# One multiply of the polynomial exponential of chunk 53 is issued behind the pair's normalisation on VectorE

## The chip, the cores and the metric

The kernel runs on one core of a Trainium2 chip. The metric is the device time of one execution in microseconds (us). A core has a matrix engine (PE in the profile), a vector engine (DVE), a scalar engine (ACT), GpSimd (POOL) and a queue engine that issues transfers (SP). Each engine runs its own instructions in the order in which they were issued, and semaphores order them between engines.

## What is computed

Attention with a soft cap on the scores, over 8 batches and 12 heads of 448 tokens with 64 dimensions, followed by a soft mixture of experts over the 3584 tokens with 768 dimensions: 32 slots, 8 experts with a hidden layer of 1024.

```python
scores = scale * np.matmul(q, k.transpose(0, 1, 3, 2))
scores = cap * np.tanh(scores / cap)
attn = np.exp(scores - max)
attn = attn / (np.sum(attn, axis=-1, keepdims=True) + 1e-09)
attn_out = np.matmul(attn, v)
...
logits = x @ phi
d = softmax(logits, over tokens); slot_input = d.T @ x
h = np.maximum(slot_input[e] @ w1[e], 0.0); slot_out[e] = h @ w2[e]
out = softmax(logits, over slots) @ slot_out
```

## The kernel before

Heads are taken in pairs, 48 in all, and four heads (two pairs) share one load of q, k and v. The scores of a pair are 7 tiles; the 336 tiles of all pairs are put into one sequence in which neighbouring pairs interleave, and the sequence is cut into 56 chunks of 6 tiles. A chunk has two halves of three tiles. For each half PE computes scores into one of two score buffers (L349), and ACT takes the tanh of them into the chunk's tile `ex` (L366, or L362 for both halves at once). Then ACT takes the exponential in place (L374), but not of all tiles: in the chunks listed in `SHARED` the first one to three tiles are left to DVE, which works out the exponential with a polynomial in seven operations.

These seven are the steps 0 to 6 of `poly_exp`: scale to a fixed-point exponent (L601), take its fraction (L603), square it (L604), scale and add (L605), multiply by the fraction (L606), add to the exponent (L607), scale to the bits of a bf16 number (L608). The steps of one chunk use a scratch tile `xf` (written by L603) and a scratch tile `xp` (written by L604 to L606). There is one of each, so chunks that are in work at the same time take turns. Chunk 52 has one such tile (448 elements), chunk 53 has three (1344), chunk 54 has one.

The place of each step on DVE is written out by hand in `POLY`: a key (j, slot) names the turn j of the main loop over chunks and a slot in it, and the value lists (chunk, step). `run(j, slot)` issues what a slot holds, first its part marked `<`, then the plain part (other work that was planned there), then the part marked `>`. One turn j of the main loop issues, in this order: slot 0, the tanh of the first half, slot m, the tanh of the second half, slot e, the exponential of chunk j - 1, then, where a pair has its last tile in chunk j - 2, the first matmuls of the probabilities with the values for that pair (`pv_first`, four of its seven tiles), slot a, the score matmuls of the next first half, slot b, the remaining matmuls and the normalisation (`pv_rest`, which calls `norm`), the cast of later values (`vcast_after`), slot c, the score matmuls of the next second half, slot d.

`norm` is a reciprocal of the row sums (L633, into `rec`) and a multiply (L636, into `xq`), both on DVE. They read the PSUM bank `pv`, of which there is one: the next pair's `pv_first` writes the same bank and waits until L636 has read it. The bank also takes filler matmuls (`spare`, `fill`) between pairs.

`vcast_after` is on GpSimd: a cast of loaded values to bf16 (L289, into `vbd`), after every other pair with a small memset (L297) ahead of it. It writes a tile that the pair's matmuls have read, so the last of these releases it, as it releases `norm`.

In turn 53 the slot '>a' holds step 5 of chunk 52 and step 2 of chunk 53 (L604), slot c holds `slot_sums` (whose DVE part is L777, into `slacc`), slot '>c' step 6 of chunk 52 and step 3 of chunk 53. Turn 54 goes on with the steps 4 and 5 of chunk 53 and the first steps of chunk 54 and closes the next pair. Turn 55 is the last; behind it a written-out sequence (`TAILSEQ`) ends the attention of the last two pairs (`pvm`, `pvl`), then come the slot sums, the two expert layers (L1071, L1099) and the output stage (L1139 to L1193), whose rows are stored by transfers that SP issues (L1127).

## Time and profile before

| | us |
|---|---|
| median of 3 runs | 283.83 |
| lowest and highest of them | 283.61, 285.08 |
| profiled execution | 282.72 |
| its span | 280.7 |

The profile shows one execution. Its span reaches from the first to the last instruction recorded; the execution's own time is 2.0 us longer. The mean granted clock of PE is 0.988 of full speed. Rows of the order of time give start, duration, engine, line, operation, output <- inputs and, in brackets, the idle time of the engine before it with what ended it. "xN" merges N instructions that follow each other. On DVE a row's duration reaches about 0.08 us into the next row. The chain of waits follows the work that ended last back to what released it.

### The profile page before, as it was taken

Reading aid. Unit: us, or ns where it says so; the run is one execution under the profiler, and the core shown is the slowest. Engines: PE = TensorE matmul, PEld = TensorE weight load, DVE = VectorE, ACT = ScalarE, POOL = GpSimd, SP = SyncE. Lnnn points to the kernel's source line nnn. Section 1 sums busy time; section 2 is a strip of 40 time slices with the busy share of each in tenths; the row PEclk is TensorE's granted clock in tenths of the full one; section 3 lists DMA queues with packets and bytes.
Section 4 is the critical chain, followed back from the end, with each engine's and each line's share of the span. In section 5 each row is a group of like instructions: output and inputs, shape, how many; then the busy total and the mean of one; then the engine's idle time right before and its main releaser. Section 6 shows DMA issues by size and latency. Waiting matters only on the chain.

```text
span 280.7 us, 10442 instructions
## 1 busy us (share of the span) xinstructions
PE 247.1 (88%) x4561; PEld 166.3 (59%) x4561; DVE 239.8 (85%) x474; ACT 248.8 (89%) x196; POOL 142.0 (51%) x198
## 2 busy tenths in 40 slices
PE   8898989998999999989999999899998989997720
PEld 6555556756675667566657675667565758652410
DVE  3479999999999999999999999999999996457840
ACT  4999999999999999999999999999999997236730
POOL 7976548663956296628663858295734120200000
PEclk9999999999999999999999999999999999999995
DMA  7999999999999999999999999999999468969997
GB/s 230 270 190 204 220 218 226 233 219 216 213 226 220 219 226 230 219 217 230 231 217 209 224 224 224 215 209 216 228 216 217 135 231 279 409 271 381 413 421 308
DMA packets 58332, 68.08 MB, mean 243 GB/s; under 512 B 4144, under 2 KB 54448, under 8 KB 58288
## 3 DMA queue, kind: packets, MB, share of 16 engines
q0 software_dynamic: 42448, 35.31, 79.7%
q1 hardware_dynamic: 15552, 31.89, 32.2%
q8 instruction: 35, 0.57, 0.7%
q10 hardware_dynamic: 288, 0.23, 0.3%
q14 instruction: 9, 0.07, 0.1%
HBM read 91.72 MB, written 19.27 MB: 395 GB/s over the span
## 4 chain that ended last, share of the span: by engine, by line
ACT 38%; DVE 31%; PE 23%; issue 4%; POOL 0%; DVEq 0%; ACTq 0%
ACT ex L366 15%; ACT ex L374 15%; PE pv L626 6%; ACT ex L362 6%; DVE xq L636 5%; DVE xp L604 4%; DVE xp L606 3%; DVE ex L607 3%; PE sc L349 2%; DVE ex L601 2%; DVE xf L603 2%; DVE ex L608 2%; DVE xp L605 2%; PE so_ps L1099 2%; DVE qT L281 2%
## 5 line engine op out<-in xcount | busy, mean ns | idle before, releaser
L366 ACT ACTIVATE ex<-sc 128x1344 f16<-128x1344 f32 (+1 forms) x87 | 112.7, 1399 | 1.4 <-PE sc L349 1.4
L374 ACT ACTIVATE ex<-ex 128x1344 bf16<-128x1344 f16 (+5 forms) x58 | 110.5, 1908 | 0.1
L626 PE MATMUL pv<-vbd,ex 128*128 128x130 bf16 (+1 forms) x1610 | 93.9, 212 | 8.7 <-DVE xq L636 4.2
L626 PEld LDWEIGHTS <-ex 128*128 128x128 bf16 (+1 forms) x1680 | 75.6, 101 | 35.8 <-issue 6.2
L289 POOL CAST vbd<-vraw 64x896 bf16<-64x896 f32 x46 | 47.6, 1034 | 56.7 <-PE pv L626 44.5
L349 PE MATMUL sc<-qT,kT 64*64 64x448 bf16 x672 | 66.1, 359 | 6.5 <-ACT ex L366 4.7
L362 ACT ACTIVATE ex<-sc 128x2688 f16<-128x2688 f32 x13 | 33.6, 2586 | 0.0
L349 PEld LDWEIGHTS <-kT 64*64 64x64 bf16 x672 | 22.0, 105 | 16.3 <-ACT ex L366 6.8
L636 DVE TENSOR_TENSOR xq<-pv,rec 128x448 bf16<-128x448 f32 x46 | 28.7, 625 | 1.6
L604 DVE TENSOR_TENSOR xp<-xf 128x1344 f16<-128x1344 uint16 (+2 forms) x34 | 27.5, 810 | 0.2
L606 DVE TENSOR_TENSOR xp<-xp,xf 128x1344 f16<-128x1344 f16 (+2 forms) x34 | 27.1, 798 | 0.6
L607 DVE TENSOR_TENSOR ex<-ex,xp 128x1344 uint16<-128x1344 uint16 (+2 forms) x34 | 26.9, 791 | 0.2
L116 POOL DMA_DIRECT2D w1b<-in_moe_w_dram x32 | 26.2, 822 | 0.0
L601 DVE TENSOR_SCALAR ex<-ex 128x1344 uint16<-128x1344 f16 (+2 forms) x34 | 16.8, 495 | 1.3 <-ACT ex L366 0.7
L297 POOL MEMSET vbd<- 64x1 bf16 x22 | 2.9, 131 | 29.7 <-PE pv L626 29.4
L281 DVE COPY kT<-kps 128x896 bf16<-128x896 bf16 x23 | 14.2, 618 | 4.2 <-PE kps L276 2.8
L605 DVE TENSOR_SCALAR xp<-xp 128x1344 f16<-128x1344 f16 (+2 forms) x34 | 17.1, 501 | 0.6
L185 POOL DMA_DIRECT2D qb<-in_q_dram x22 | 16.3, 739 | 2.5 <-PE qps L279 1.8
L603 DVE TENSOR_SCALAR xf<-ex 128x1344 uint16<-128x1344 uint16 (+2 forms) x34 | 16.7, 491 | 0.4
L608 DVE TENSOR_SCALAR ex<-ex 128x1344 uint16<-128x1344 uint16 (+2 forms) x34 | 16.4, 483 | 0.4
L120 POOL DMA_DIRECT2D w2d<-in_moe_w_dram x21 | 16.4, 817 | 0.0
L185 POOL DMA_DIRECT2D kb<-in_k_dram x22 | 16.3, 742 | 0.0
(124 smaller groups left out, 320.1 us busy)
## 6 DMA issues: line engine op xcount, KB each, us to landing
w1b<-in_moe_w_dram POOLq DMA_DIRECT2D x32, 384.0 KB, 9.6
vraw<-in_v_dram SPq DMA_DIRECT2D x44, 224.0 KB, 6.2
w2d<-in_moe_w_dram POOLq DMA_DIRECT2D x21, 384.0 KB, 9.5
w2t<-w2d SPq DMA_DIRECT2D x21, 384.0 KB, 6.7
out_dram<-ob SPq DMA_DIRECT2D x7, 768.0 KB, 6.6
qb<-in_q_dram POOLq DMA_DIRECT2D x22, 224.0 KB, 7.3
kb<-in_k_dram POOLq DMA_DIRECT2D x22, 224.0 KB, 7.7
w2b<-in_moe_w_dram POOLq DMA_DIRECT2D x11, 384.0 KB, 9.1
```

Of the source, the lines that this page charges most:

```text
L116: pool.dma_start(out=w1b[e][:, js, fs], in_=w1r[:, e, js, fs])
L185: pool.dma_start(out=t, in_=quad_ap(nm, Q))
L289: pool.tensor_copy(vbds[Q % 2][r, :, :, c0:c0 + DH], raw[r])
L349: ins = pe.matmul(sc[cs, u, 0:S], qkT["k", Q][r, c, cs], qkT["q", Q][r, :, cs], start=True, stop=True).ins
L362: apart["t", i - 1] = apart["t", i] = act.activation(exs[j].bitcast(F16), own["board"][:, :, 0:S], ACT.Tanh, scale=qk_scale / cap).ins
L366: ins = act.activation(exs[j][:, half * CS + u0:half * CS + u1, :].bitcast(F16), (own[0] if i == u0 == 0 else sc)[:, u0:u1, 0:S], ACT.Tanh ...
L374: act.activation(exs[j][:, u0:u1, :], exs[j][:, u0:u1, :].bitcast(F16), ACT.Exp, scale=cap)
L604: lambda: dve.tensor_tensor(p, s, s.bitcast(F16), op=ALU.mult),
L606: lambda: dve.tensor_tensor(p, p, s, op=ALU.mult),
L607: lambda: dve.tensor_tensor(y, y, p, op=ALU.add),
L626: pe.matmul(out_, exs[j][r, u, q0:q0 + (HP if tail else P)], v_, start=(c == 0 and g == gs[0] < NF), stop=(c == NT - 1), skip_group_check= ...
L636: dve.tensor_tensor(xq[Q][:, h, s0:s1, :], pv[:, 0:s1 - s0, 0:DH], rec.to_broadcast([P, s1 - s0, DH]), op=ALU.mult)
```

## The change

Step 2 of chunk 53 (the square, L604, on 128 partitions by 1344 elements) moves from slot '>a' to slot '<c' of turn 53, that is from ahead of `pv_rest` to behind it. The other entries stay.

```diff
             (53, 'm'): ((53, 0),),
             (53, 'e'): ((52, 3), (51, 6)),
             (53, '<a'): ((52, 4), (53, 1)),
-            (53, '>a'): ((52, 5), (53, 2)),
+            (53, '>a'): ((52, 5),),
+            (53, '<c'): ((53, 2),),
             (53, '>c'): ((52, 6), (53, 3)),
             (54, '<a'): ((53, 4),),
```

On DVE the order around it becomes:

```
before: L603 (53), L607 (52), L604 (53), L633, L636, L777, L608 (52), L605 (53), L606 (53)
after:  L603 (53), L607 (52), L633, L636, L604 (53), L777, L608 (52), L605 (53), L606 (53)
```

The numbers in brackets are chunks. The other engines and the transfer queues keep their order, and no wait between engines changes.

## The prediction

> **What bounds the kernel now.** I read first the busy rows of the page and the stretches of the end, then the chain of waits, then the time order of each engine around the edited place.

> ```profile
> span 280.7 us, 10442 instructions
> ...
> PE 247.1 (88%) x4561; PEld 166.3 (59%) x4561; DVE 239.8 (85%) x474; ACT 248.8 (89%) x196; POOL 142.0 (51%) x198
> ```

> ```profile
> 220.00:224.00 4.00, 3.94 (x83) 2.82 (x84) 3.90 (x12) 4.00 (x5) 1.05 (x2) 1.00 0.33 98
> 224.00:228.00 4.00, 2.95 (x73) 2.34 (x73) 3.90 (x9) 4.00 (x4) 0.93 (x1) 1.00 0.73 241
> 228.00:232.00 4.00, 3.94 (x62) 2.72 (x61) 3.92 (x10) 3.70 (x3) 1.11 (x2) 1.00 0.68 226
> 232.00:236.00 4.00, 4.00 (x92) 3.52 (x89) 3.03 (x10) 3.81 (x5) 0.00 (x0) 1.00 0.90 304
> ```

> Columns: stretch, length, busy time of PE, its weight loads, DVE, ACT and POOL, granted clock, DMA share, GB/s. Over the whole span three engines are nearly level, so the shares decide nothing. The edited operation runs in the second stretch, where PE does 2.95 us of work in 4 and DVE and ACT are full; before and after it PE is full. The granted clock is 1.00 throughout, so no clock term enters the sum. The chain of waits says what costs PE that time:

> ```profile
> 224.05 0.31 DVE ex L607
> ...
> 224.38 1.60 DVE xp L604
> 225.98 0.13 DVE rec L633
> ...
> 226.13 0.63 DVE xq L636
> 226.77 0.14 issue
> 226.91 0.84 PE pv L626 x12
> ```

> ```profile
> 223.33 0.90 PE L626 MATMUL pv<-vbd,ex 128*128 128x130 bf16 x15
> ...
> 225.29 0.57 PE L349 MATMUL sc<-qT,kT 64*64 64x448 bf16 x6
> 226.91 0.84 PE L626 MATMUL pv<-vbd,ex 128*128 128x130 bf16 x12 [1.05 <-DVE xq L636]
> ```

> The chain runs on DVE up to 226.77 and on PE from then on. At the crossing PE has finished its score matmuls (225.29 + 0.57 = 225.86) and stands still for 1.05 us: the next pair's matmuls need the bank pv, which the normalisation (rec, then xq) must have read. The bank was complete at 223.33 + 0.90 = 224.23, but rec came only at 225.9, because the edited operation, the multiply L604 of chunk 53, stood before it for 1.60 us. That duration is odd:

> ```profile
> L604 DVE TENSOR_TENSOR xp<-xf x34: 386/847/1599, 14.2 to 231.4; 128x1344 f16<-128x1344 uint16 x27, 128x896 f16<-128x896 uint16 x5, 128x448 f16<-128x448 uint16 x2
> ```

> ```profile
> 224.35 0.93 POOL L289 CAST vbd<-vraw 64x896 bf16<-64x896 f32 x1 [3.13 <-PE pv L626]
> ```

> The median of L604 is 0.85 us and this is the slowest of 34. GpSimd's cast of the values began at 224.35, 0.03 us ahead of it, and ended at 225.28; L604 ended 0.70 us behind that, about as if it had begun when the cast ended. Other meetings of the two kinds:

> ```profile
> 138.31 0.85 DVE L604 TENSOR_TENSOR xp<-xf 128x1344 f16<-128x1344 uint16 x1
> ...
> 212.50 1.07 DVE L606 TENSOR_TENSOR xp<-xp,xf 128x1344 f16<-128x1344 f16 x1
> ```

> ```profile
> 138.67 1.27 POOL L289 CAST vbd<-vraw 64x896 bf16<-64x896 f32 x1 [2.17 <-PE pv L626]
> ...
> 211.90 0.95 POOL L289 CAST vbd<-vraw 64x896 bf16<-64x896 f32 x1
> ```

> Where the multiply is already running (138.31), it keeps its 0.85 us and the cast takes 1.27; where the cast runs first (211.90 to 212.85), the multiply's end slips to 0.72 us behind the cast's end. So whichever starts first makes the other wait. The normalisation is not held by a cast: the last matmul of a pair releases both, so they meet again and again, as at 229.94 and 229.79 in rows further down, and yet the page's group of L636 has the mean 625 ns over 46.

> ```profile
> L636 DVE TENSOR_TENSOR xq<-pv,rec 128x448 bf16<-128x448 f32 x46 | 28.7, 625 | 1.6
> ```

> [...]

> **The change, part by part.** Nothing is added or removed: L604 of chunk 53 moves on DVE past rec (L633) and xq (L636) and comes ahead of slacc (L777). PE, ACT, GpSimd and the DMA queues keep their order; no DMA is moved or passed.

> ```profile
> 225.91 0.19 DVE L633 RECIPROCAL rec<-pv 128x7 f32<-128x7 f32 x1
> 226.13 0.62 DVE L636 TENSOR_TENSOR xq<-pv,rec 128x448 bf16<-128x448 f32 x1
> 226.68 0.38 DVE L777 TENSOR_TENSOR slacc<-slps,slacc 128x224 f32<-128x224 f32 x1
> ```

> (1) The normalisation. Its wait for PE was over at 224.23 and DVE is free at 224.36, so rec starts at 224.38 instead of 225.91: 1.53 us earlier. xq ends at 226.75 - 1.53 = 225.22. With the 0.14 to 0.16 us from xq's end to the first matmul, the bank is free for PE at about 225.38, before PE is done with its scores at 225.86. PE's 1.05 us go down to the 0.05 or so between two of its groups: pv starts near 225.9, 1.0 us earlier.

> (2) The multiply. Behind xq it starts near 225.14, while the cast runs until 225.28; 0.70 us behind that is 225.98, or 0.85 us by itself is 225.99. So slacc, which followed the normalisation at 226.68, now follows L604 at about 225.91, and all later work on DVE has 0.77 us in hand. Bounds of this term: 0 if L604 were held for 1.60 us again, 0.77 if not. I take 0.77, since only 0.14 us of the cast are left.

> (3) What comes back. DVE gains 0.77, PE 1.0. They meet first at the next normalisation, behind which the filler matmul and the last pairs write the same bank:

> ```profile
> 228.66 0.85 DVE L607 TENSOR_TENSOR ex<-ex,xp 128x1344 uint16<-128x1344 uint16 x1
> 229.42 0.27 DVE L603 TENSOR_SCALAR xf<-ex 128x448 uint16<-128x448 uint16 x1
> 229.70 0.21 DVE L633 RECIPROCAL rec<-pv 128x7 f32<-128x7 f32 x1
> 229.94 0.62 DVE L636 TENSOR_TENSOR xq<-pv,rec 128x448 bf16<-128x448 f32 x1
> ```

> ```profile
> 230.85 0.28 PE junk L875
> ...
> 231.18 0.84 PE pv L626 x12
> ```

> xq ends at 230.56 and frees the bank for 230.70; the chain has the filler at 230.85, so the slack is 0.15. With PE 1.0 and DVE 0.77 earlier, PE waits 1.0 - 0.77 - 0.15 = 0.08 us. PE keeps about 0.9.

> (4) ScalarE. It is full but for one idle of 0.30 us, which ends at the scores that PE now gives earlier:

> ```profile
> 228.87 1.29 ACT L366 ACTIVATE ex<-sc 128x1344 f16<-128x1344 f32 x1 [0.30 <-PE sc L349]
> ...
> 233.18 2.63 ACT L374 ACTIVATE ex<-ex 128x1344 bf16<-128x1344 f16 x3
> ```

> ```profile
> 236.22 0.86 PE L626 MATMUL pvl<-vbd,ex 128*128 128x130 bf16 x12
> ```

> So the last exponential ends at 235.81 - 0.30 = 235.51. PE uses its tile from the fifth of those twelve matmuls, at 236.22 + 4/12 x 0.86 = 236.5. Against 235.81 that leaves 0.7, with 0.1 for the signal 0.6; with the 0.30 ScalarE allows PE 0.9 us. If it did not gain its 0.30, PE would keep 0.6.

> (5) To the end. From 226.91 to the output stage the chain is PE without a gap, and the last stage writes at the rate of the DMA engines:

> ```profile
> 265.00:270.00 5.00, 3.23 (x16) 1.43 (x15) 2.92 (x4) 3.08 (x4) 0.00 (x0) 1.00 1.02 424
> 270.00:275.00 5.00, 0.00 (x0) 0.00 (x0) 1.45 (x2) 0.41 (x1) 0.00 (x0) 0.90 1.01 420
> ```

> A full write stage (424, 420 GB/s) does not shrink, but it starts when PE delivers, so it moves as a whole. Sum: -1.0 + 0.1 = -0.9 us. The profiled execution took 282.72 us (span 280.7 and 2.0 around it), so its own sum is 281.8. It lies 1.1 us under the median of the runs, 283.83; the same 0.9 us off the median gives **282.9 us**. The gain can't exceed PE's idle of 1.05 us, 0.37%.

> **Rivals.** (a) The stall moves to the next cast (slower). This cast follows a small memset, both released by PE's last matmul of the pair:

> ```profile
> 229.57 0.16 POOL L297 MEMSET vbd<- 64x1 bf16 x1 [4.30 <-PE pv L626]
> 229.79 0.95 POOL L289 CAST vbd<-vraw 64x896 bf16<-64x896 f32 x1
> ```

> Today L603 (229.42) starts well ahead of the cast (229.79). With GpSimd 1.0 and DVE 0.77 earlier, L603 comes at 228.65 and the cast at 228.79 or a little before: the lead shrinks from 0.37 to 0.14 us, and to nothing if the memset no longer stretches. If the cast wins, L603 waits for its end near 229.7 and ends about 229.97; rec and xq then end near 230.8, 0.2 us later than today. The 1.0 us are lost and PE is 0.1 us late, or 0.3 if the cast itself starts late behind L607: 283.9 to 284.1 us. Against it: L603 still leads by the rows. [...]

> (b) The stall is a coin flip. Cast and L604 start 0.03 us apart. In executions where L604 wins, the kernel before has L604 for 0.85 us, xq ends near 226.0 and PE waits 226.15 - 225.86 = 0.3 us only; the change is then worth 0.3: 283.5 us. For it: the 0.03 us; against: both starts hang on the same earlier DVE results, and the profiled run, which has the stall, is no slower than the others.

> (c) The change does nothing: DVE's order is kept in sum, and a wait behind xq takes its place, ScalarE's for example if its idle of 0.30 remains and a later one appears: 283.8. The 0.6 us of slack in (4) speak against it.

> (d) PE keeps all of its 1.05 us, and the tail gets ScalarE's 0.30 on top: 1.35, so 282.5. Against it: from 226.91 the chain is on PE, not on ScalarE, and the tail's links from PE to a small copy and back shift and do not shrink.

> **How the numbers follow.** Forecast 0.50, (a) 0.20, (b) 0.15, (c) 0.07, (d) 0.08. The likeliest gives 282.9, by itself 282.2 to 283.4. For 8 in 10 the range must reach (b) and most of (a) above and (d) below, and the runs of one kernel spread by 1.5 us (283.61 to 285.08): 281.8 to 284.2. About 0.5% (1.4 us) is what a measurement of this kernel can tell from no change, and the whole mechanism is worth less than that; so within 0.5% gets 0.70. Faster by more than 0.5% needs (d), or the forecast with a low median: 0.22. Slower by more needs (a) with a high median: 0.08.

> **What would show it.** Right: L604 of chunk 53 takes about 0.85 us and ends near 226.0; rec follows the short L607 without delay; PE's idle of 1.05 before pv is gone; ACT's idle of 0.30 is gone; the first store starts 0.9 us earlier. Wrong: L603 of chunk 54 or another operation takes over 1 us beside the cast near 228.8 (rival a); PE waits elsewhere for the same time (c); the first store shifts by over 1.1 us (d).

## The result and the profile after

| | before | after |
|---|---|---|
| median of the runs | 284.74 us (16 runs, 282.72 to 288.16) | 282.07 us (16 runs, 281.52 to 283.81) |
| profiled execution, its span | 282.72, 280.7 us | 282.33, 280.2 us |
| ratio | | 0.9935, interval 0.9913 to 0.9957 |

Ratios leave out disturbed executions, here the longest ones of a kernel; medians count all. The gain, 0.65%, is larger than the mechanism of the prediction allows (0.37% at most), while the two profiled executions differ by only 0.39 us. Both need an explanation. First the rows of the place itself, from the page, the view of the edited line and the time order of DVE after the change (every line number behind the edit is one higher):

```profile
span 280.2 us, 10442 instructions
...
PE 247.4 (88%) x4561; PEld 166.2 (59%) x4561; DVE 239.1 (85%) x474; ACT 248.8 (89%) x196; POOL 142.1 (51%) x198
```

```profile
L605 DVE TENSOR_TENSOR xp<-xf x34: 386/848/909, 14.2 to 230.5; 128x1344 f16<-128x1344 uint16 x27, 128x896 f16<-128x896 uint16 x5, 128x448 f16<-128x448 uint16 x2
```

```profile
224.27 0.20 DVE L634 RECIPROCAL rec<-pv 128x7 f32<-128x7 f32 x1
224.51 0.62 DVE L637 TENSOR_TENSOR xq<-pv,rec 128x448 bf16<-128x448 f32 x1
225.05 0.91 DVE L605 TENSOR_TENSOR xp<-xf 128x1344 f16<-128x1344 uint16 x1
225.88 0.38 DVE L778 TENSOR_TENSOR slacc<-slps,slacc 128x224 f32<-128x224 f32 x1
...
228.63 0.27 DVE L604 TENSOR_SCALAR xf<-ex 128x448 uint16<-128x448 uint16 x1
```

The slowest of the 34 squares now takes 0.91 us, where it took 1.60. The normalisation comes 1.64 us earlier (224.27 against 225.91), `slacc` 0.80 us earlier (225.88 against 226.68). GpSimd's casts and PE beside it, in time order:

```profile
224.32 0.93 POOL L289 CAST vbd<-vraw 64x896 bf16<-64x896 f32 x1 [3.13 <-PE pv L627]
228.45 0.10 POOL L297 MEMSET vbd<- 64x1 bf16 x1 [3.20 <-PE pv L627]
228.61 1.11 POOL L289 CAST vbd<-vraw 64x896 bf16<-64x896 f32 x1
```

```profile
223.31 0.90 PE L627 MATMUL pv<-vbd,ex 128*128 128x130 bf16 x15
...
225.27 0.57 PE L349 MATMUL sc<-qT,kT 64*64 64x448 bf16 x6
225.77 0.86 PE L627 MATMUL pv<-vbd,ex 128*128 128x130 bf16 x12
...
239.62 4.07 PE L1072 MATMUL hp<-w1b,slT 128*32 128x512 bf16 x72
...
247.42 1.15 PE L1100 MATMUL so_ps<-w2t,hpad 128*32 128x384 bf16 x23
248.75 0.82 PE L1100 MATMUL so_ps<-w2t,hpad 128*32 128x384 bf16 x13 [0.19 <-issue]
249.51 0.50 PE L1140 MATMUL op<-so,ET 128*128 128x384 bf16 x2
```

The next pair's `pv` follows the scores without idle time. A useful measure for every run below is the distance from the start of the last `pv` group before the place (x15) to the first matmuls of the expert layer (`hp`): here 239.62 - 223.31 = 16.31 us. Before the change the time order of PE has:

```profile
240.56 4.07 PE L1071 MATMUL hp<-w1b,slT 128*32 128x512 bf16 x72
...
248.36 1.64 PE L1099 MATMUL so_ps<-w2t,hpad 128*32 128x384 bf16 x36
249.93 0.50 PE L1139 MATMUL op<-so,ET 128*128 128x384 bf16 x2
```

There it is 240.56 - 223.33 = 17.23. So PE gains 0.92 us up to the expert layers. Then it gives half back: after 23 of the 36 matmuls with `w2t` the changed kernel's PE stands until 248.75, and `op` comes only 0.42 us earlier (249.51 against 249.93). The stretches of the end show the same from the side of the engines (length, then busy PE, weight loads, DVE, ACT, POOL, granted clock, DMA share, GB/s), after and before:

```profile
224.00:228.00 4.00, 4.00 (x89) 3.08 (x90) 3.93 (x11) 4.00 (x4) 0.93 (x1) 1.00 0.76 258
...
245.00:250.00 5.00, 4.81 (x110) 2.61 (x105) 1.94 (x9) 1.07 (x3) 0.00 (x0) 1.00 0.67 262
```

```profile
245.00:250.00 5.00, 5.00 (x137) 3.43 (x130) 2.43 (x10) 1.32 (x3) 0.00 (x0) 1.00 0.91 357
```

PE is full at the place (4.00 of 4, it was 2.95), and has a hole of 0.19 us by 250 that the kernel before lacks. The waits of SP's transfer queue in the window from 216 to 252 us say for what (total, times, longest), after and before:

```profile
SPq L1051 <- DMA w2t<-w2d: 4.1, 4, 2.2
```

```profile
SPq L1050 <- DMA w2t<-w2d: 2.7, 4, 0.8
```

SP waits 1.4 us longer for these transfers, and the last of the 21 is issued at 243.4 us, against 242.8 before. So the second layer's weights did not move forward with PE. The row of PE names no releaser of its hole (`issue`); that it is these weights is the reading that fits, and no run shows it apart. In this pair of executions 0.5 us of span are left of 0.92.

### The profile page after: what moved, and what is told of

It reads as the page before. It is cut to its first block, busy times and chain, and to the rows that moved or that the text cites. A ratio compares the mean times of both kernels' runs of the same rounds, so it can differ in the third digit from the quotient of the medians.

```text
span 280.2 us, 10442 instructions
## 1 busy us (share of the span) xinstructions
PE 247.4 (88%) x4561; PEld 166.2 (59%) x4561; DVE 239.1 (85%) x474; ACT 248.8 (89%) x196; POOL 142.1 (51%) x198
## 4 chain that ended last, share of the span: by engine, by line
ACT 38%; DVE 27%; PE 27%; issue 4%; POOL 1%; DVEq 0%; ACTq 0%
ACT ex L366 15%; ACT ex L374 15%; PE pv L627 8%; ACT ex L362 6%; DVE xq L637 4%; PE sc L349 3%; DVE xp L605 3%; DVE xp L607 3%; DVE ex L608 2%; PE so_ps L1100 2%; DVE ex L602 2%; PE hp L1072 2%; DVE xp L606 2%; DVE xf L604 2%; DVE ex L609 2%
## 5 line engine op out<-in xcount | busy, mean ns | idle before, releaser
L366 ACT ACTIVATE ex<-sc 128x1344 f16<-128x1344 f32 (+1 forms) x87 | 113.0, 1403 | 1.1 <-PE sc L349 1.1
L374 ACT ACTIVATE ex<-ex 128x1344 bf16<-128x1344 f16 (+5 forms) x58 | 110.7, 1916 | 0.1
L289 POOL CAST vbd<-vraw 64x896 bf16<-64x896 f32 x46 | 47.3, 1027 | 57.6 <-PE pv L627 38.5
L349 PE MATMUL sc<-qT,kT 64*64 64x448 bf16 x672 | 66.1, 359 | 6.6 <-ACT ex L366 4.7
L349 PEld LDWEIGHTS <-kT 64*64 64x64 bf16 x672 | 22.0, 105 | 16.4 <-ACT ex L366 6.9
L637 DVE TENSOR_TENSOR xq<-pv,rec 128x448 bf16<-128x448 f32 x46 | 28.7, 625 | 1.6
L607 DVE TENSOR_TENSOR xp<-xp,xf 128x1344 f16<-128x1344 f16 (+2 forms) x34 | 27.1, 798 | 0.6
L605 DVE TENSOR_TENSOR xp<-xf 128x1344 f16<-128x1344 uint16 (+2 forms) x34 | 26.8, 790 | 0.2
L606 DVE TENSOR_SCALAR xp<-xp 128x1344 f16<-128x1344 f16 (+2 forms) x34 | 17.3, 507 | 0.6
L281 DVE COPY kT<-kps 128x896 bf16<-128x896 bf16 x23 | 14.2, 618 | 4.1 <-PE kps L276 2.8
L297 POOL MEMSET vbd<- 64x1 bf16 x22 | 2.8, 129 | 28.4 <-PE pv L627 28.2
L604 DVE TENSOR_SCALAR xf<-ex 128x1344 uint16<-128x1344 uint16 (+2 forms) x34 | 16.7, 492 | 0.4
```

Of the source, the lines that this page charges most:

```text
L289: pool.tensor_copy(vbds[Q % 2][r, :, :, c0:c0 + DH], raw[r])
L349: ins = pe.matmul(sc[cs, u, 0:S], qkT["k", Q][r, c, cs], qkT["q", Q][r, :, cs], start=True, stop=True).ins
L366: ins = act.activation(exs[j][:, half * CS + u0:half * CS + u1, :].bitcast(F16), (own[0] if i == u0 == 0 else sc)[:, u0:u1, 0:S], ACT.Tanh ...
L374: act.activation(exs[j][:, u0:u1, :], exs[j][:, u0:u1, :].bitcast(F16), ACT.Exp, scale=cap)
L605: lambda: dve.tensor_tensor(p, s, s.bitcast(F16), op=ALU.mult),
L607: lambda: dve.tensor_tensor(p, p, s, op=ALU.mult),
```

## Experiments

**Theory** (L below): the square is held by GpSimd's cast (1.60 us against a median of 0.85); moving it takes away PE's idle of 1.05 us, and by some other effect the runs gain more than the profiled pair. **Rivals**: the stall is a coin flip of single executions; the gain comes from DVE's new order and not from the hold; part of the gain lies at a place that one profile may not show (S below), above all in the granted clock (theory C below).

**The kernel before, profiled again** (no edit).

> The kernel before once more, unchanged, with a profile of another execution. Theory L (the stall alone): the trace again shows L604 of chunk 53 at about 1.6 us and PE idle for about 1.05 us ahead of the matmuls of the next pair, and nothing else that the changed kernel lacks; its time lies within 0.3% of the runs of before, and the kernel before is about 0.3% slower than the changed one. Rival S (a second loss): the profiled execution of before was the fastest of 16, so most executions lose another 1 to 4 us at a place that its profile did not show. Then this profile, if it is of a slower execution, shows a further gap on PE after 227 us, or a granted clock under 1.00 in some stretch after 224 us.

Measured: 283.62 us median of 12, ratio 0.9997 (0.9963 to 1.0030). DVE in time order:

```profile
224.79 1.60 DVE L604 TENSOR_TENSOR xp<-xf 128x1344 f16<-128x1344 uint16 x1
```

The stall is there again, 1.60 us. In all eight profiles of the old order with the cast at its place (three more of the kernel before, the two that fill PE's idle and the one with the square issued twice stand below) the cast starts 0.03 to 0.05 us ahead of the square and holds it (1.59 to 1.60 us, and 2.48 for the two squares). So the coin flip falls. But the 12 executions, of one kernel on one chip, reach from 282.45 to 287.32 us.

**The changed kernel again** (no edit; run beside two different sets of the kernel before).

> The changed kernel once more, unchanged. Theory L: ratio to before 0.997 (0.9 us), PE 0.9 us earlier at the first expert layer in the trace and at the end. Rival S: ratio 0.993 or lower again, with a smaller spread of its runs than those of before. The second loss seen in the changed kernel's first profile (PE waits some 0.5 us in the second expert layer at 248 us, where its weights arrive by transfer) is there again if the transfers set the end there; if it is a chance of that execution, it is gone and the end moves by 0.9 us.

> The changed kernel, unchanged, as the measure for the next run on the same chip: 282.1 to 282.5 us, ratio to before 0.993 to 0.995, no execution above 284 us.

Measured: 282.46 us, ratio 0.9949 (0.9922 to 0.9976), and 282.16 us, ratio 0.9949 (0.9924 to 0.9974). The ratio lies between the marks of the two theories (0.997, and 0.993 or lower). The distance is 16.31 and 16.32 us. The first shows the hole in the second layer again:

```profile
249.61 0.82 PE L1100 MATMUL so_ps<-w2t,hpad 128*32 128x384 bf16 x13 [0.34 <-issue]
```

**The order of before, but the cast later.** GpSimd first clears the tile that the cast then overwrites, so the cast begins 0.9 us later and DVE's order stays:

```diff
         elif h == 1 and Q + 2 < NQ:
+            if pr == 43:
+                pool.memset(vbds[Q % 2][0:HP, :, :, 0:DH], 0.0)
             vcast(Q + 2, 0)
```

> The order of the kernel before, but GpSimd first clears the part of the tile that its cast then writes (the cast overwrites it), so that the cast begins about 0.9 us later, when the multiply is over. [...] Rival: a memset holds VectorE as the cast does; then the multiply takes 1.6 us or more and the ratio is 1.000 or above. Rival: the position of the multiply ahead of rec alone costs the time, whatever its length; then PE's idle stays near 1 us.

Under theory L the square takes 0.85 us instead of 1.60, so `xq` comes 0.75 us earlier and PE's idle falls from 1.05 to about 0.3 us; an estimate from these is 0.75 us or a little less of 283.65, a ratio of 0.997 to 0.998. Measured: 282.78 us, ratio 0.9956 (0.9930 to 0.9983), a little under that. GpSimd, DVE and PE in time order (this kernel's numbers are two higher than those of before):

```profile
225.47 0.84 POOL L301 MEMSET vbd<- 64x896 bf16 x1 [3.13 <-PE pv L628]
226.38 0.92 POOL L289 CAST vbd<-vraw 64x896 bf16<-64x896 f32 x1
```

```profile
225.51 0.86 DVE L606 TENSOR_TENSOR xp<-xf 128x1344 f16<-128x1344 uint16 x1
```

```profile
224.46 0.90 PE L628 MATMUL pv<-vbd,ex 128*128 128x130 bf16 x15
...
227.29 0.84 PE L628 MATMUL pv<-vbd,ex 128*128 128x130 bf16 x12 [0.31 <-POOL vbd L289]
...
240.95 4.07 PE L1073 MATMUL hp<-w1b,slT 128*32 128x512 bf16 x72
```

A memset starts 0.04 us ahead of the square and does not hold it: 0.86 us. With a cast at that distance it took 1.60. So the cast is the cause, not the place in DVE's order, and most of the gain comes without the move. PE idles 0.31 us, for the later cast now; the distance is 16.49.

**More idle time.** Step 2 of chunk 53 issued twice at its old place (the second square writes the same values):

```diff
-            (53, '>a'): ((52, 5), (53, 2)),
+            (53, '>a'): ((52, 5), (53, 2), (53, 2)),
```

> The kernel before with L604 of chunk 53 issued twice in a row (the second writes the same values), so that rec starts 0.85 us later and PE stands still for about 1.9 us instead of 1.05. Theory L: 0.85 us slower than before, 284.5 us, clocks as in before. Theory C: the chance of a lower clock grows with the idle; more than half of the executions are under 0.983, many at 0.965 to 0.98, the median is 286 to 288 us (ratio 1.007 or above), and the profile shows a stretch after 227 us with a granted clock under 1.00 and matmuls that take longer there.

Measured: 288.61 us, ratio 1.0105 (1.0025 to 1.0185). The median is 0.6 us above the range of theory C; against the 284.69 of the kernel before beside it, 0.9 us more of DVE work cost almost 4 us. Of six executions five took 288.0 us or more, at mean clocks of 0.960 to 0.970, and one 284.30 at 0.987. PE in time order and stretches of the profiled one:

```profile
224.55 0.90 PE L626 MATMUL pv<-vbd,ex 128*128 128x130 bf16 x15
...
229.02 0.84 PE L626 MATMUL pv<-vbd,ex 128*128 128x130 bf16 x12 [1.95 <-DVE xq L636]
...
246.96 4.07 PE L1071 MATMUL hp<-w1b,slT 128*32 128x512 bf16 x72
```

```profile
230.00:239.00 9.00, 8.94 (x88) 6.01 (x86) 5.61 (x14) 6.99 (x6) 1.05 (x2) 0.50 0.55 177
...
240.00:241.00 1.00, 1.00 (x19) 1.00 (x18) 0.21 (x1) 0.00 (x0) 0.00 (x0) 0.95 1.03 375
```

After an idle of 1.95 us PE's granted clock is 0.50 for some 10 us. The distance is 22.41 us, 5.18 more than 17.23, of which the second square is 0.90. The question is then whether the 1.05 us of the kernel before do the same in some executions.

**Three more profiles of the kernel before** (no edit).

> The kernel before, unchanged, for the profile of one more execution; three of them go together. Theory C: an execution at 285 us or more shows PE's granted clock at 0.50 for some us, beginning within about 3 us behind the idle of 1.05 us, and matmuls of twice the length there; an execution near 283 us shows 1.00 throughout up to 270 us.

> As the first look. Rival to theory C: the executions of 284 to 286 us have a clock of 1.00 up to 270 us, and what is longer in them is the last landing of the output stores: in the profile of the filled kernel one transfer engine was still at work at 18 to 25 GB/s for 1.3 us when the others were done.

> As the first and the second look: where an execution is longer than 283.5 us, the stretches tell which of the two it is, clock or last store.

Measured: 284.32, 282.72 and 288.44 us. The second is like the first profile, clock 1.00 all through the place, distance 17.24. The first, in time order and stretches:

```profile
223.68 0.90 PE L626 MATMUL pv<-vbd,ex 128*128 128x130 bf16 x15
...
227.26 1.36 PE L626 MATMUL pv<-vbd,ex 128*128 128x130 bf16 x12 [1.05 <-DVE xq L636]
...
229.28 1.30 PE L349 MATMUL sc<-qT,kT 64*64 64x448 bf16 x5
...
242.44 4.07 PE L1071 MATMUL hp<-w1b,slT 128*32 128x512 bf16 x72
```

```profile
227.50:228.00 0.50, 0.50 (x8) 0.50 (x6) 0.50 (x2) 0.50 (x2) 0.00 (x0) 0.50 0.35 141
...
230.50:231.00 0.50, 0.50 (x8) 0.49 (x8) 0.00 (x0) 0.38 (x1) 0.00 (x0) 0.69 1.01 197
231.00:232.00 1.00, 1.00 (x24) 0.75 (x23) 0.39 (x2) 1.00 (x2) 0.49 (x2) 1.00 0.96 350
```

Right behind the idle of 1.05 us the clock falls to 0.50, from 227.4 to 230.8, some 3.4 us. Five score matmuls take 1.30 us; at full clock (after the change, 226.98) the same five take 0.73. The distance is 242.44 - 223.68 = 18.76, or 1.53 us more than 17.23. The third profile, the same views:

```profile
223.88 0.90 PE L626 MATMUL pv<-vbd,ex 128*128 128x130 bf16 x15
...
227.46 0.96 PE L626 MATMUL pv<-vbd,ex 128*128 128x130 bf16 x12 [1.05 <-DVE xq L636]
...
245.39 4.07 PE L1071 MATMUL hp<-w1b,slT 128*32 128x512 bf16 x72
```

```profile
228.00:238.00 10.00, 9.94 (x104) 6.96 (x102) 6.01 (x15) 8.16 (x7) 1.05 (x2) 0.50 0.52 174
238.00:239.00 1.00, 1.00 (x17) 1.00 (x17) 0.83 (x2) 0.00 (x0) 0.00 (x0) 0.86 0.84 310
```

Half clock for some 10.2 us; the distance is 21.51, or 4.28 us more. The stall and the idle are alike in all five profiles of the kernel before (1.59 to 1.60 and 1.05 us); what differs is whether and how long the clock falls behind it.

**Fill the idle, keep the stall.** 36 matmuls of 57 columns (then, in a second kernel, 8 of 288 columns) on ones go into columns of the slot sums' bank that nothing reads, at the point where PE idles; `slacc` comes two DVE operations later.

```diff
...
+    def fill_late(n):
+        for _ in range(n):
+            pe.matmul(late["bank"][:, NT * W:], ones, ones[:, 0:512 - NT * W], start=False, stop=True,
+                      skip_group_check=True)
+        dve.tensor_tensor(slacc, late["sums"], slacc, op=ALU.add)
...
+    at(53, "d", fill_late, 36)
```

> The kernel before with the stall kept, but PE's idle of 1.05 us filled: 36 matmuls on ones into unused columns of the bank of the slot sums run behind the score matmuls (about 27 ns each, 0.97 us in all), and slacc comes two operations later on DVE. What it tells apart: of 41 executions of the kernel before, 17 had a mean granted clock under 0.983 and a median of 285.4 us, the other 24 had 0.983 to 0.988 and 283.2 us, while none of the 24 of the changed kernel and of the late cast was under 0.983. Theory C (PE's idle now and then costs clock as well): the fill takes no work off the chain, yet no execution falls under 0.983, and the median is near 283.2 us, ratio to before 0.996 to 0.998. Theory L (only the stalled time counts): the clocks scatter as in the kernel before, 4 in 10 of them under 0.983, and the ratio is 1.000.

> The filled kernel with 8 matmuls of 288 columns in place of 36 of 57 (about 0.12 us each, 0.97 us in all), so that the program has 16 more PE instructions instead of 72. The stall of VectorE is kept and the chain is that of the kernel before. Theory C: PE is busy through the stall, so no execution falls to half clock behind it; all lie where the undisturbed executions of before do, 282.5 to 284 us, none above 284.5, and the median is about 283.2 us, while the runs of before beside them again reach 285 to 288. Theory L: the spread up to 288 us stays, since the stall stays. If the first filled kernel was 1 us slower than the undisturbed executions because of its own extra instructions, that is gone here; if it is still there, the fill itself costs it.

Measured: 284.38 us, ratio 1.0010 (0.9983 to 1.0038), and 284.24 us, ratio 1.0019 (0.9998 to 1.0039). PE in time order, the second kernel:

```profile
223.78 0.90 PE L626 MATMUL pv<-vbd,ex 128*128 128x130 bf16 x15
...
226.24 1.15 PE L795 MATMUL slps<-ones 128*128 128x288 bf16 x8
227.36 0.84 PE L626 MATMUL pv<-vbd,ex 128*128 128x130 bf16 x12
...
241.01 4.07 PE L1086 MATMUL hp<-w1b,slT 128*32 128x512 bf16 x72
...
250.09 1.15 PE L1114 MATMUL so_ps<-w2t,hpad 128*32 128x384 bf16 x21 [0.46 <-issue]
```

No idle is left in front of `pv`. The distance in the second kernel is 17.23, to the hundredth that of before, so its chain up to the expert layers keeps its length; in the first it is 17.49, 0.26 us more. The spread is narrow: all 24 executions lie between 283.97 and 285.47, where the kernel before reached 287.91 beside them. This speaks for the idle as the cause of the long falls, but weakly, since one in ten of the kernel before would be two or three in 24. Two signs of theory C on record failed: 12 of the 24 executions have a mean clock under 0.983, and the median did not fall to 283.2. The filled kernels lie about 1 us above the undisturbed executions of before (283.19 in the table below), in the second kernel with a wait for `w2t` behind the chain (row 250.09). The time is not lost to a fall of the clock in their two profiles, where it is 1.00 until 271.8 and 275.4 us, behind PE's last matmul. Both end instead with about 1.5 us in which the transfers move only 6 to 49 GB/s, from 279.5 to 281.1 and from 280.0 to 281.6 us, behind some 400 GB/s; the three profiles of before with an undisturbed clock have no such end. Why the fill makes the second layer's weights or the last stores later was not found, so these two runs do not price the clock.

**Use the hole in the second layer.** The changed kernel with two output tiles one step earlier, near where PE waits for `w2t` (run twice):

```diff
-        if n0 % 8 == 4 and n0 > 4 and done < NH:
+        if n0 % 8 == 4 and done < NH:
```

> The changed kernel, with the pairs of output tiles that are woven into the second half of the second expert layer beginning one step of eight earlier. In both profiles of the changed kernel PE waits 0.5 us in that layer near 249 us for weights that a transfer brings, so that 0.44 us of its gain were left at 250 us of 0.94 at 240. If the transfers are what takes the gain back, PE has the output tiles to do in the wait: 0.2 to 0.5 us below the changed kernel (ratio to before 0.993). If the wait only moves (the copy of the first half of the layer's result is needed for those tiles and ends about when the weights land), the time is that of the changed kernel, ratio 0.994 to 0.995.

> The changed kernel with the output tiles one step earlier, once more, beside the changed kernel itself. Its trace ended 59.68 us behind the cast of the values of the turn before, the changed kernel's two traces 59.96 and 60.36 us. If that is the wait for the transferred weights, filled, it is 0.2 to 0.6 us faster than the changed kernel in the same call (281.7 to 282.1 us); if it was chance, the two medians lie within 0.15 us.

Measured: 282.34 us, ratio 0.9948 (0.9919 to 0.9977), and 282.58 us, ratio 0.9948 (0.9922 to 0.9974). Beside the second the changed kernel itself had 0.9949. There is no difference. But the edit does not fill the hole: PE waits behind the 23rd of the matmuls with `w2t`, and the tiles now come behind the 28th instead of the 36th. PE of the second of these runs in time order:

```profile
247.33 1.15 PE L1100 MATMUL so_ps<-w2t,hpad 128*32 128x384 bf16 x23
249.27 0.50 PE L1100 MATMUL so_ps<-w2t,hpad 128*32 128x384 bf16 x5 [0.79 <-issue]
```

The hole is 0.79 us there and still ahead of the tiles. So these two runs don't price it.

**The executions of the kernel before, by their mean clock.** Every execution comes with its mean granted clock, except the 16 of before in the result, which are left out here. PE's clock also falls behind its last matmul (in the profile of before to 0.50 at 274.0 us; in the stretch 270 to 275 us that the prediction shows it is 0.90 on average), so an execution without any other fall has 0.982 to 0.988, by when that one begins; a fall of 3.4 us in 282 costs another 0.5 x 3.4 / 282 = 0.006, one of 10.2 us 0.018.

| kernel, mean clock | executions | median us | lowest, highest |
|---|---|---|---|
| before, 0.983 and more | 49 | 283.19 | 282.45, 284.74 |
| before, 0.978 to 0.982 | 38 | 284.87 | 282.84, 286.82 |
| before, 0.970 and less | 10 | 287.56 | 287.01, 288.44 |
| after, 0.982 to 0.988 | 40 | 282.25 | 281.52, 283.81 |
| cast later, 0.983 to 0.988 | 12 | 282.78 | 281.86, 283.33 |

The groups of before stand 1.68 and 4.37 us above the first; the profiles gave 1.53 and 4.28 for the two falls. About half of its executions have one. A few near 0.982 can be in the wrong group. In the filled kernels, which end later, the clock is 0.980 to 0.986 and the time does not go with it (medians 284.40 below 0.983, 284.21 above). The profile of the first has the mean 0.981 and no fall before the end, so there a low mean is the end's and not a fall's.

**Where the falls begin and end.** The traces list each moment at which the granted clock changes. In all 14 profiles of this case the stretches between two changes are whole multiples of 3.413 us: at half clock 3.413 and 10.240 (1 and 3 of them), at full clock 37.547, 40.960 and 44.373 between a fall and the one at the end (11, 12 and 13), and 221.866 to 269.653 ahead of the first (65 to 79). So in these profiles the clock changed on a grid of 3.413 us, and the grid can be carried back from the end to the idle of every profile:

| profile | PE idle | stretch of the grid | PE busy in it, us | clock behind it |
|---|---|---|---|---|
| before, first of the three | 226.21 to 227.26 | 223.98 to 227.39 | 2.36 | 0.50 |
| before, third of the three | 226.41 to 227.46 | 224.63 to 228.04 | 2.36 | 0.50 |
| square issued twice | 227.07 to 229.02 | 226.46 to 229.87 | 1.47 | 0.50 |
| before, profiled again | 226.26 to 227.31 | 225.78 to 229.19 | 2.36 | 1.00 |
| before | 225.86 to 226.91 | 222.85 to 226.26, 226.26 to 229.68 | 3.01, 2.77 | 1.00 |
| before, second of the three | 225.97 to 227.02 | 222.90 to 226.31, 226.31 to 229.72 | 3.07, 2.71 | 1.00 |
| idle filled, 36 matmuls | filled | 224.01 to 227.42 | 3.41 | 1.00 |
| idle filled, 8 matmuls | filled | 224.22 to 227.63 | 3.41 | 1.00 |

The three falls begin at the first grid point behind the idle, 0.13, 0.58 and 0.85 us after it. In the two profiles in which a grid point splits the idle, none follows. In the filled kernels the grid lies to the place almost as in the first row, PE is busy there, and none follows. "Profiled again" has the whole idle in one stretch and PE as busy as in the first two rows, yet no fall; what else counts stays open.

## Why the prediction came out

**(1) The normalisation** was sized right: 1.53 us earlier forecast, 1.64 measured, and PE's idle of 1.05 us is gone.

**(2) The multiply**: 0.85 us to 225.99 forecast, 0.91 to 225.96 measured; DVE gains 0.80 against 0.77.

**(3) and (4) What comes back**: PE was to keep about 0.9 us and has 0.92 at `hp`. ScalarE's idle of 0.30 us is gone and its last exponential ends at 235.38 (0.1 earlier than forecast); the order of time of ACT after the change:

```profile
228.35 1.38 ACT L366 ACTIVATE ex<-sc 128x1344 f16<-128x1344 f32 x1
...
232.65 2.73 ACT L374 ACTIVATE ex<-ex 128x1344 bf16<-128x1344 f16 x3
```

**(5) "It moves as a whole"** failed in the profiled pair: 0.42 of 0.92 us are left at the first output tile and at the first store (issued at 250.49 against 250.91), it seems because the transfers of `w2t` did not move with PE. The two other profiles of the changed kernel have 0.25 and 0.61 us left at the first output tile, against 26.60 us from the last `pv` group to it in the kernel before. Over the executions the medians fit the forecast nevertheless: the undisturbed ones of before have 283.19, all of after 282.25, which is 0.94 us, the forecast 0.9. Where the half that the profiles mostly miss at the output tile comes back was not traced, so part of this agreement may be luck.

**The step that was wrong** is "the granted clock is 1.00 throughout, so no clock term enters the sum", and with it the bound that the gain can't exceed PE's idle. It holds for the profiled execution up to PE's last matmul, and that execution was the fastest of its 16. In about half of the executions the idle that the change removes is followed by half clock. By the means: 284.40 for all 97 of before, 282.38 for all 40 of after, so 2.02 us, of which 283.28 - 282.35 = 0.93 is between the executions at 0.983 and above, and the other 1.1 the falls, (38 x 1.71 + 10 x 4.32) / 97 = 1.12. The ratios still count the middle group, hence 0.9935 to 0.9949 where the stall alone gives 1 - 0.94 / 283.19 = 0.9967. So the time, 282.07, lies in the forecast's range and 0.8 us under its value, for a reason that it excluded. That it lies so near is luck in part: the base of the forecast, 283.83 from three runs, is 0.9 us under the 284.74 of all 16 and so holds little of the falls. The chance of "within 0.5%", 0.70, was too high for the same reason.

That the fall comes from the idle rests on the order in time (it starts behind the idle in each of three profiles), on its going when the idle goes in two unlike ways (by the mean clocks none of 40 with the move, where one of 0.982 is at the border, and none of 12 with the later cast, which keeps 0.31 us), on the two filled profiles, and on five of six executions with 1.95 us. Why 1.05 us do it in one execution and not in the next is shown in part: the fall begins and ends on the grid of 3.413 us, and it came only where the idle lay whole in one stretch of it. If the grid lies anywhere with equal chance, an estimate from 48 falls in 97 executions is that the next grid point must come within about 48 / 97 x 3.41 = 1.7 us behind the idle, which the profiles fit (0.13 and 0.58 us fell, 1.88 us did not); no run set the place of the grid on purpose.

**The rivals.** (a) fell: L604 of chunk 54 (228.63; L603 in the lines of before) kept its 0.27 us, 0.02 us behind the cast (228.61), and the cast took longer instead (1.11 us against 0.95). The rows don't order the two closer than that, and the forecast lead of 0.14 us was gone. That this operation would wait for a whole cast was the author's estimate; the longest of its 34 takes 0.59 us before the change and 0.60 after. (b) fell: the stall is in all eight profiles with the old order and the cast at its place. (c) fell, but for the hole in the second layer. (d) fell at its place: PE did not keep its full 1.05, and the extra came from the clock.

## What to carry to other kernels

Where a VectorE operation and a GpSimd cast start at nearly the same time (here 0.03 us apart, and the square took 1.60 us instead of 0.85), see which starts first, and put what the critical path waits for ahead of the loser if the trace shows that the cast does not hold it, as here the normalisation (`xq` from `pv` takes 0.62 to 0.63 us in all 46 rows of before). A short idle of PE in a full stretch cost more than its length here: 1.05 us cost 0.9 us by itself and 1.1 us more on average. So list the time and the mean clock of many executions before one profile at full clock is taken for all. When a chain gets earlier, see whether the transfers that it meets later do too.
